# Two tiles share the weight tiles of a second layer as these are made, and a pair of tiles gets eight load buffers

## The chip, the cores and the metric

The kernel runs on one core of a Trainium2 chip. The metric is the device time of one execution in microseconds (us), smaller is better. The kernel before was timed in three runs; one further execution was recorded by the profiler, and all rows below are from it. Engines: PE is TensorE (matmuls), DVE is VectorE, ACT is ScalarE, POOL is GpSimd, and SP issues nearly all DMAs.

## The reference

Chunked attention over 8 x 8 heads of 576 positions, its 4608 tokens of 512 features, and then two dense two-layer networks, one after the other:

```python
scores = np.matmul(q_c, k_c.transpose(0, 1, 2, 4, 3)) / np.sqrt(D)     # chunks of 64
attn = np.exp(scores - np.max(scores, axis=-1, keepdims=True))
out = np.matmul(attn / (np.sum(attn, axis=-1, keepdims=True) + 1e-09), v_c)
x = out.transpose(0, 2, 1, 3).reshape(B * S, H * D)                     # 4608 x 512
h = x @ w_in                                                            # 512 -> 2048
x = (np.maximum(h, 0.0) + alpha * np.minimum(h, 0.0)) @ w_out           # 2048 -> 512
g = x @ w_gate                                                          # 512 -> 1536
y = (g * (1.0 / (1.0 + np.exp(-g))) * (x @ w_val)) @ w_out2             # 1536 -> 512
```

## The kernel before

**Tiles and products.** The 4608 tokens are nine tiles of 512. An operand in f32 is split into a high and a low part, and a product takes three matmuls of 128 x 512 (`mm3`). Weights come in a wide form; `convert` loads one block into a `raw` buffer and rebuilds it in a buffer `c` (one ACT and three DVE instructions), `whole` and `make` split it into the parts that matmuls read (buffers `w`, or `cw` for halves), and `Layer.put` stores these in DRAM (`l_in`, `l_out`, `l_b`, `l_out2`), from where `Layer.get` and `load` bring them back for later tiles. Two tiles together, a pair, are multiplied by seven products of half the size each way instead of eight (`layer1`, `layer2`); these need sums of blocks of the weights (made by `sums`, parts 5, 6, 3, 7) and sums and differences of blocks of the input (made by `operands`). A tile alone uses `plain1` and `plain2`.

**Stages**, in the order of the code and with their time in the profiled execution: attention of the first tiles (0 to 88 us); the first layer of tiles 0 and 1, `plain1` (to 181); the second layer of tile 0, `plain2`, which makes the tiles of w_out, stores them, and writes the rebuilt blocks to `cd` (to 228); the second layer of tile 1 with the stored tiles (to 276); layer 1 of pair (2,3), `mlp_a(2)` (to some 385), while `out_sums` reads `cd` back and makes the sums for w_out; layer 2 of that pair, `mlp_a2(2)` (to 495); tile 8 alone (to some 611); pair (4,5) (to 780), with `out2_quad` making the parts of w_out2; the second network for tile 0 (to 885), for the pairs (1,2) (to 1067) and (3,4) (to 1274); pair (6,7) of the first network (to 1435); the second network for (5,6) (to 1623) and (7,8). Attention of later tiles (`heads`) lies beside the matmuls of these stages.

**What sets the order.** A planner, `Program.order`, gives each instruction a place on its engine from written costs, dependencies and due times; matmuls of the products keep the order of the code ("main" items), everything else is put where a due time and free buffers allow. `after=` holds an item back until a named item has been placed. The engines then run their lists in order and wait by semaphores.

**Buffers that matter here.** `h`: 2, for activations, and for results on their way to `x2d` (`to_x2`). `t`: 5, for sums, for `t = x12 - x11` in `operands`, and for chunks of output on their way to DRAM (`e` in `to_out`). `c`: 3, for rebuilt weight blocks. `raw`: 2 double buffers, whose four halves also serve as load buffers. `xin`: 4 load buffers. `xin8` is `xin` with the halves of `raw`: 8. `w`: 7 whole weight tiles. PSUM banks: X0, X1, W0, W1, Y0, Y1, a0, a1.

**Steps that the change touches.** `operands` (L479) loads the blocks of a pair into `ring` and makes 14 operands `op` (each an ACT copy and a DVE difference). With a ring of 4 it does the whole of kt = 0 and then kt = 1; with 8 it loads the upper blocks of both first. Only the calls with `xin8` have 8: `mlp_b` and `mlp_a(6)`. `to_out` (L765) collects four blocks of a tile, transposes them on PE into banks a0 and a1 in four chunks of 128 tokens, copies each chunk to a buffer `e` and stores it. `to_x2` (L714) copies or adds a result into `h` and stores it. L229 is the copy in `copy_`, L234 the add in `add2`, L526 to L528 are the three matmuls of `mm3`: one line for many places, so the names of the tiles tell them apart.

Of the kernel before, what the change touches and what calls it, by code (L numbers as in the profile page):

```python
# [17 lines left out]
P = 128  # L18
# [123 lines left out]
def attention_moe_moe2(ctx, tc, q, k, v, w_in, w_out, alpha, w_gate, w_val, w_out2, out):  # L142
# [31 lines left out]
    NB = 512  # L174
# [44 lines left out]
    cd = dram.tile([4 * JA, P, NB], F32, name="cd")  # L219
# [78 lines left out]
    def convert(src, into=None):  # L298
# [7 lines left out]
        dma(NB * 8 * P, lambda: nsp.dma_start(out=dst, in_=src), [], rk)  # L306
# [172 lines left out]
    def operands(xd, name, i, ring):  # L479
# [169 lines left out]
    def plain2(js, col, banks, weights, natural=False):  # L649

        for m in range(2 * js):
            j, r = divmod(m, 2)
            c = 2 * r + col
            t, tk = ops.next()
            split(t[:, 0], t[:, 1], gts[j][c], NB, [("g", j, c)], tk + (0,), tk + (1,))
            w, wkeys = weights(m)

            def go(t=t, w=w, m=m):
                first, stop = m == 0, m == 2 * js - 1
                for a, b in enumerate(banks):  # L660
                    if natural:
                        acc = bank[b].rearrange("p (a f) -> p a f", a=2)
                        for i, (gp, wp) in enumerate(((0, 0), (0, 1), (1, 0))):
                            npe.matmul(out=acc, lhsT=t[:, gp, a * P:(a + 1) * P], rhs=w[:, :, wp, :],
                                       start=first and i == 0, stop=stop and i == 2, skip_group_check=True)
                    else:
                        mm3(bank[b], w[:, a // 2], t, slice((a % 2) * P, (a % 2 + 1) * P), NB, first, stop)
            item("PE", 12 * (NB + 32) / 2400, go, [*wkeys, tk + (0,), tk + (1,)], list(banks), main=True, lat=0.25)
# [340 lines left out]
```

## Time and profile before

| | us |
|---|---|
| median of 3 runs | 1816.07 |
| lowest and highest of them | 1810.56, 1817.45 |
| the profiled execution, its own time | 1815.11 |
| its span, first to last instruction | 1813.3 |
| PE busy in the span | 1689.6 |
| DVE busy | 1213.0 |
| ACT busy | 941.6 |
| mean granted clock of PE | 0.972 |

Busy time is a sum over the whole span; a stage that is bound by another engine or by a load shows only in the views by stretch. A clock of 1.00 is 2.4 GHz, 0.50 is 1.2 GHz; a value between is the mean over a stretch. In a timeline the bracket at a row's end is how long the engine had been idle before it and which instruction or transfer ended last before it started. Names such as `op<-xin` stand for a written tile and the tile that it is made from.

### The profile page before, as it was taken

The numbers are of one execution on the slowest core, as the hardware profiler recorded it, in microseconds if no ns is written. First come the engines' busy times: TensorE is split into PE (matmuls) and PEld (weight loads), VectorE is DVE, ScalarE is ACT, GpSimd is POOL, SyncE is SP. The second block draws the span as 40 slices with busy tenths as digits, with TensorE's granted clock in tenths as the row PEclk, the third lists the DMA queues.
The fourth block names the chain that finished last, engine by engine and source line by source line (L and its number), as shares of the span: only waits on it lengthen the run. The fifth ranks groups of instructions, "written<-read, shape, count | busy, mean of one in ns | idle before, by whom it ended". The sixth has DMA issues, their size and how long they took to land. (4 is left out here: it accounts for less than half of the span.)

```text
span 1813.3 us, 26654 instructions
## 1 busy us (share of the span) xinstructions
PE 1689.6 (93%) x9388; PEld 1365.9 (75%) x9388; DVE 1213.0 (67%) x2155; ACT 941.6 (52%) x1651; POOL 1.0 (0%) x8
## 2 busy tenths in 40 slices
PE   7998997879989799999899999999999799999998
PEld 6777876747767587878688778778778688778876
DVE  5787836789767688866576844587678444754473
ACT  5667525765354577544444542574675332643352
POOL 0000000000000000000000000000000000000000
PEclk8999998989989899999999999999999899999999
DMA  8879997988999995778665566896655665555553
GB/s 184 251 258 253 333 317 229 305 283 245 260 234 315 345 319 182 274 261 275 230 210 186 197 209 210 223 239 218 215 186 203 221 219 192 187 199 193 190 189 122
DMA packets 330805, 424.37 MB, mean 234 GB/s; under 512 B 176304, under 2 KB 196784, under 8 KB 330672
## 3 DMA queue, kind: packets, MB, share of 16 engines
q1 hardware_dynamic: 328608, 422.67, 73.1%
q8 instruction: 74, 1.21, 0.3%
q14 instruction: 59, 0.48, 0.1%
q10 hardware_dynamic: 2064, 0.01, 0.1%
HBM read 319.82 MB, written 102.76 MB: 233 GB/s over the span
## 5 line engine op out<-in xcount | busy, mean ns | idle before, releaser
L526 PE MATMUL X<-op,w 128*128 128x512 f32 x1056 | 422.8, 400 | 38.6 <-DVE h L234 11.1
L528 PE MATMUL X<-op,w 128*128 128x512 f32 x1056 | 415.8, 394 | 1.1 <-DVE op L234 1.1
L527 PE MATMUL X<-op,w 128*128 128x512 f32 x1056 | 415.4, 393 | 0.0
L229 ACT ACTIVATE op<-g 128x512 fp32r<-128x512 f32 x348 | 210.7, 629 | 135.6 <-PE X L527 47.3
L526 PEld LDWEIGHTS X<-op,w 128*128 128x128 f32 x1056 | 200.7, 190 | 94.5 <-ACT s L229 16.6
L234 DVE TENSOR_TENSOR op<-g,op 128x512 fp32r<-128x512 f32 x348 | 226.9, 685 | 36.6 <-ACT op L229 30.6
L526 PE MATMUL W<-op,w 128*128 128x512 f32 x544 | 216.6, 398 | 26.5 <-ACT op L229 12.0
L526 PE MATMUL Y<-op,w 128*128 128x512 f32 x560 | 226.2, 404 | 11.8 <-ACT h L698 7.7
L528 PEld LDWEIGHTS X<-op,w 128*128 128x128 f32 x1056 | 200.5, 190 | 45.1 <-DVE op L234 2.3
L527 PEld LDWEIGHTS X<-op,w 128*128 128x128 f32 x1056 | 201.1, 190 | 39.7
L528 PE MATMUL Y<-op,w 128*128 128x512 f32 x560 | 221.2, 395 | 0.0
L527 PE MATMUL Y<-op,w 128*128 128x512 f32 x560 | 221.1, 395 | 0.0
L528 PE MATMUL W<-op,w 128*128 128x512 f32 x544 | 215.7, 397 | 0.4 <-DVE op L234 0.4
L527 PE MATMUL W<-op,w 128*128 128x512 f32 x544 | 214.5, 394 | 0.0
L229 ACT ACTIVATE s<-X 128x512 f32<-128x512 f32 x172 | 102.6, 597 | 106.0 <-PE X L528 104.4
L234 DVE TENSOR_TENSOR h<-Y,s 128x512 f32<-128x512 f32 x78 | 53.7, 690 | 136.7 <-PE Y L528 136.5
L526 PEld LDWEIGHTS W<-op,w 128*128 128x128 f32 x544 | 103.6, 190 | 51.7 <-ACT op L229 14.9
L526 PEld LDWEIGHTS Y<-op,w 128*128 128x128 f32 x560 | 107.6, 192 | 36.8 <-ACT h L698 8.8
L706 DVE SCALAR_TENSOR_TENSOR g<-h,nalpha_sb,g 128x512 f32<-128x512 f32 x144 | 107.3, 747 | 33.9 <-ACT h L698 33.3
L528 PEld LDWEIGHTS Y<-op,w 128*128 128x128 f32 x560 | 106.9, 191 | 23.3
L527 PEld LDWEIGHTS Y<-op,w 128*128 128x128 f32 x560 | 107.5, 192 | 21.6
L528 PEld LDWEIGHTS W<-op,w 128*128 128x128 f32 x544 | 103.6, 190 | 25.7 <-DVE op L234 4.0
(127 smaller groups left out, 2024.0 us busy)
## 6 DMA issues: line engine op xcount, KB each, us to landing
w<-l_out SPq DMA_DIRECT2D x168, 512.0 KB, 3.6
w<-l_b SPq DMA_DIRECT2D x126, 512.0 KB, 4.3
w<-l_in SPq DMA_DIRECT2D x56, 512.0 KB, 4.3
w<-l_out SPq DMA_DIRECT2D x88, 256.0 KB, 5.3
l_b<-w SPq DMA_DIRECT2D x84, 256.0 KB, 3.4
l_out<-cw SPq DMA_DIRECT2D x80, 256.0 KB, 4.6
l_in<-w SPq DMA_DIRECT2D x64, 256.0 KB, 4.8
raw<-in_moe_w_out_dram SPq DMA_DIRECT2D x28, 512.0 KB, 5.5
```

The costliest lines, as they stand in the source:

```text
L229: pr.add([("ACT", act(n), lambda: na.activation(out=dst, in_=src, func=AF.Copy), False), ("DVE", dvep(n) if psum else dve1(n), lambda: nv. ...
L234: item("DVE", dve2(n), lambda: nv.tensor_tensor(out=dst, in0=a, in1=b, op=op), reads, writes, **kw)
L526: npe.matmul(out=acc, lhsT=w[:, 0, wk], rhs=x[:, 0, :n], start=first, stop=False, skip_group_check=True)
L527: npe.matmul(out=acc, lhsT=w[:, 1, wk], rhs=x[:, 0, :n], start=False, stop=False, skip_group_check=True)
L528: npe.matmul(out=acc, lhsT=w[:, 0, wk], rhs=x[:, 1, :n], start=False, stop=stop, skip_group_check=True)
L706: nv.scalar_tensor_tensor(out=g, in0=h, scalar=nal, in1=g, op0=ALU.mult, op1=ALU.add)
```

## The change

- `plain2` takes a list of columns. For each weight tile it issues the matmuls of tile 0 (banks X0, X1, W0, W1) and then those of tile 1 (banks Y0, Y1, a0, a1). The second pass over stored tiles for tile 1 is gone, with its 32 loads of 256 KB.
- The new `out_tile` converts two blocks of w_out, splits and stores them, and makes the sums 5, 6, 3, 7 at once from the blocks while they are in `c`. `out_sums` is gone, and so are the 16 writes to and 16 reads from `cd` for w_out (256 KB each); `cd` has half the size.
- `operands` always loads the upper blocks of both kt first, and every pair uses the ring of 8.
- A pair is a tuple of tiles. The second network now takes (1,2), (3,4), (5,8), (6,7).
- Chunks of output go through the 3 buffers `c` instead of the 5 buffers `t`.
- `out2_quad` holds its loads back until given main items are placed: four quads in the stage of tile 8, two in layer 1 of pair (4,5).

```diff
-    def operands(xd, name, i, ring):
+    def operands(xd, name, pair, ring):
...
-            dma(NB * 4 * P, lambda: nsp.dma_start(out=t, in_=xd[:, f, (i + c) * NB:(i + c + 1) * NB]),
-                [(name, i + c, f)], [key])
+            dma(NB * 4 * P, lambda: nsp.dma_start(out=t, in_=xd[:, f, pair[c] * NB:(pair[c] + 1) * NB]),
+                [(name, pair[c], f)], [key])
...
-        if ring.n == 4:
-            for kt in range(KD // 2):
-                lower(kt, *upper(kt))
-        else:
-            up = [upper(kt) for kt in range(KD // 2)]
-            for kt in range(KD // 2):
-                lower(kt, *up[kt])
+        up = [upper(kt) for kt in range(KD // 2)]
+        for kt in range(KD // 2):
+            lower(kt, *up[kt])
...
-    def plain2(js, col, banks, weights, natural=False):
+    def plain2(js, cols_, weights, natural=False):
...
             j, r = divmod(m, 2)
-            c = 2 * r + col
-            t, tk = ops.next()
-            split(t[:, 0], t[:, 1], gts[j][c], NB, [("g", j, c)], tk + (0,), tk + (1,))
             w, wkeys = weights(m)
+            for col, banks in cols_:
+                c = 2 * r + col
+                t, tk = ops.next()
+                split(t[:, 0], t[:, 1], gts[j][c], NB, [("g", j, c)], tk + (0,), tk + (1,))
...
-            e, ek = tring.next()
+            e, ek = cs.next()
             copy_(e[:w], bank[bk][:w], NB, [], [ek, bk])
...
-    def out_sums(j):
-        bl = sums(*old_tiles(2 * JA + 2 * j), False)
-        for p in (5, 6, 3, 7):
-            make(lay_out, (j, p), bl[p], chalves.next())
-
-    def out2_quad(j):
-        c = [z for m in (2 * j, 2 * j + 1) for z in convert(rows(w_out2, m))]
+    def out_tile(m, ahead={}):
+
+        j, r = divmod(m, 2)
+        if not r:
+            c = [convert(rows(w_out, 2 * j + i)) for i in range(2)]
+            for i in range(2):
+                ahead[2 * j + i] = t, keys = whole(*c[i])
+                for h, p in enumerate(OUT[i]):
+                    lay_out.put((j, p), t[:, h], keys[h])
+            bl = sums(*c[0], *c[1], False)
+            for p in (5, 6, 3, 7):
+                make(lay_out, (j, p), bl[p], chalves.next())
+        return ahead[m]
+
+    def out2_quad(j, after):
+        c = [z for m in (2 * j, 2 * j + 1) for z in convert(rows(w_out2, m), after=pr.mains[after])]
...
-        plain2(JA, 0, XW, partial(new_tile, lay_out, OUT, lambda j: j, partial(rows, w_out), base=2 * JA))
+        plain2(JA, [(0, XW), (1, YA)], out_tile)
         evict_x2(XW, 0)
-        plain2(JA, 1, YX, partial(stored, lay_out, OUT, lambda j: j))
-        evict_x2(YX, 1)
+        evict_x2(YA, 1)
...
-        mlp_a(2, second_quads(lay_in, lambda x: old_tiles(2 * x[1])))
+        mlp_a((2, 3), second_quads(lay_in, lambda x: old_tiles(2 * x[1])))
         heads(8, m0, 14)
-        for j in range(JA):
-            out_sums(j)
-        mlp_a2(2)
+        mlp_a2((2, 3))
...
-        for j in range(JB):
-            out2_quad(j)
-        mlp_a(4, got_in)
-        mlp_a2(4)
+        for j in range(4):
+            out2_quad(j, m0 + 6 * j)
+        m0 = len(pr.mains)
+        mlp_a((4, 5), got_in)
+        for j in range(4, JB):
+            out2_quad(j, m0 + 20 * (j - 4))
+        mlp_a2((4, 5))
...
-        mlp_b(5, got_b)
-        mlp_b(7, got_b)
+        mlp_b((5, 8), got_b)
+        mlp_b((6, 7), got_b)
```

**The order on ACT, at the start of pair (2,3).** In a row the number at the end of a name is the buffer. Before, results `h` of tile 1 are copied between operands `op` that are made from loads `xin`:

```order
L229 ACTIVATE w_5_135<-t_2_127 128x256
L229 ACTIVATE op_5_72<-xin_3_116 128x512
L229 ACTIVATE s_0_117<-W0_159 128x512
L229 ACTIVATE w_6_136<-t_3_128 128x256
L229 ACTIVATE h_0_123<-X0_157 128x512
L229 ACTIVATE op_7_74<-xin_2_115 128x512
L229 ACTIVATE op_9_76<-xin_1_114 128x512
L229 ACTIVATE h_1_124<-X1_158 128x512
L229 ACTIVATE op_3_70<-xin_0_113 128x512
L229 ACTIVATE s_1_118<-X0_157 128x512
```

After, the place where the results of tile 0 are copied out of X0 to W1:

```order
L229 ACTIVATE op_8_75<-xin_1_114 128x512
L229 ACTIVATE op_9_76<-xin_3_116 128x512
L229 ACTIVATE h_0_123<-X0_157 128x512
L229 ACTIVATE h_1_124<-X1_158 128x512
L229 ACTIVATE w_0_130<-t_2_127 128x256
L229 ACTIVATE op_10_77<-raw_0_139 128x512
L229 ACTIVATE w_1_131<-t_2_127 128x256
L229 ACTIVATE op_11_78<-raw_1_140 128x512
L229 ACTIVATE w_2_132<-t_3_128 128x256
L229 ACTIVATE h_0_123<-W0_159 128x512
L229 ACTIVATE h_1_124<-W1_160 128x512
L229 ACTIVATE w_3_133<-t_3_128 128x256
```

The operands that stood between the copies of X0 and the first `s` have moved ahead of these copies, and they are made from `raw` as well as `xin`.

**The order on ACT, at the end of pair (3,4) or (5,6) of the second network and the start of the next.** Before, at the end of (5,6):

```order
L229 ACTIVATE t_1_126<-a1_164 128x512
L229 ACTIVATE t_2_127<-a0_163 128x512
L229 ACTIVATE g6_3_108<-X1_158 128x512
L229 ACTIVATE t_3_128<-a1_164 128x512
L229 ACTIVATE t_4_129<-a0_163 128x512
L229 ACTIVATE t_0_125<-a1_164 128x512
L229 ACTIVATE t_1_126<-a0_163 128x512
L229 ACTIVATE t_2_127<-a1_164 128x512
L229 ACTIVATE op_6_73<-t_3_128 128x512
L229 ACTIVATE op_7_74<-t_4_129 128x512
L229 ACTIVATE op_2_69<-xin_1_114 128x512
L229 ACTIVATE op_3_70<-xin_3_116 128x512
```

After, at the end of (5,8):

```order
L229 ACTIVATE op_4_71<-raw_0_139 128x512
L229 ACTIVATE g6_2_107<-X0_157 128x512
L229 ACTIVATE g6_3_108<-X1_158 128x512
L229 ACTIVATE op_5_72<-raw_1_140 128x512
L229 ACTIVATE s_0_117<-W0_159 128x512
L229 ACTIVATE s_1_118<-X0_157 128x512
L229 ACTIVATE c_2_143<-a0_163 128x512
L229 ACTIVATE c_0_141<-a1_164 128x512
L229 ACTIVATE s_2_119<-X0_157 128x512
L732 ACTIVATE g0_0_81<-h_0_123 128x512
L732 ACTIVATE g0_1_82<-h_1_124 128x512
```

The operands `op` stand ahead of the copies out of a0 and a1; the copies write `c`, and there are two in place of eight before the next layer's `g`.

**The order on ACT, at the end of the kernel.** Before:

```order
L229 ACTIVATE g6_2_107<-X0_157 128x512
L229 ACTIVATE t_1_126<-a0_163 128x512
L229 ACTIVATE t_2_127<-a1_164 128x512
L229 ACTIVATE t_3_128<-a0_163 128x512
L229 ACTIVATE t_4_129<-a1_164 128x512
L229 ACTIVATE t_0_125<-a0_163 128x512
L229 ACTIVATE t_1_126<-a1_164 128x512
L229 ACTIVATE t_2_127<-a0_163 128x512
L229 ACTIVATE t_3_128<-a1_164 128x512
```

After:

```order
L229 ACTIVATE c_2_143<-a0_163 128x512
L229 ACTIVATE c_0_141<-a1_164 128x512
L229 ACTIVATE c_1_142<-a0_163 128x512
L229 ACTIVATE g6_2_107<-X0_157 128x512
L229 ACTIVATE g6_3_108<-X1_158 128x512
L229 ACTIVATE c_2_143<-a1_164 128x512
L229 ACTIVATE c_0_141<-a0_163 128x512
L229 ACTIVATE c_1_142<-a1_164 128x512
L229 ACTIVATE c_2_143<-a0_163 128x512
L229 ACTIVATE c_0_141<-a1_164 128x512
L229 ACTIVATE c_1_142<-a0_163 128x512
L229 ACTIVATE c_2_143<-a1_164 128x512
```

Ten copies through three buffers stand where eight went through five.

## Rows read from the trace of the kernel before

**Rows 1.** The page, part 1: busy time, share of the span, instructions.

```profile
PE 1689.6 (93%) x9388; PEld 1365.9 (75%) x9388; DVE 1213.0 (67%) x2155; ACT 941.6 (52%) x1651; POOL 1.0 (0%) x8
```

**Rows 2.** Stretches: from:to, length, busy by engine (x), PE clock, DMA share, GB/s.

```profile
181.00:228.00 47.00, 45.24 (x240) 37.26 (x234) 37.90 (x68) 25.35 (x45) 0.00 (x0) 1.00 0.98 336
228.00:276.00 48.00, 46.93 (x234) 38.16 (x234) 16.98 (x34) 11.53 (x23) 0.00 (x0) 1.00 0.93 312
276.00:310.00 34.00, 25.60 (x92) 19.48 (x91) 22.02 (x43) 20.64 (x41) 0.00 (x0) 0.80 0.76 233
310.00:380.00 70.00, 57.11 (x266) 45.16 (x266) 56.24 (x126) 51.07 (x108) 0.00 (x0) 0.96 0.93 303
380.00:410.00 30.00, 24.63 (x155) 16.71 (x157) 26.01 (x52) 17.28 (x34) 0.00 (x0) 0.86 0.83 250
400.00:450.00 50.00, 47.84 (x357) 36.89 (x348) 47.26 (x86) 28.87 (x49) 0.00 (x0) 1.00 0.75 221
495.00:535.00 40.00, 34.07 (x224) 26.90 (x224) 28.63 (x56) 22.91 (x46) 0.00 (x0) 0.91 0.92 224
535.00:600.00 65.00, 59.10 (x446) 46.72 (x446) 46.39 (x100) 28.27 (x59) 0.00 (x0) 0.97 1.00 313
600.00:622.00 22.00, 13.33 (x42) 9.86 (x42) 18.37 (x33) 12.64 (x24) 0.00 (x0) 0.77 0.97 349
```

**Rows 3.** Timeline of PE: start, us, instruction, [idle before <- ended by].

```profile
283.69 0.80 PE L526 MATMUL X<-op,w 128*128 128x512 f32 x1 [7.19 <-ACT h L229]
...
600.14 0.80 PE L526 MATMUL W<-op,w 128*128 128x512 f32 x1 [2.35 <-DMA w<-l_out]
...
617.45 0.80 PE L526 MATMUL W<-op,w 128*128 128x512 f32 x1 [6.84 <-ACT h L229]
...
885.28 0.80 PE L526 MATMUL W<-op,w 128*128 128x512 f32 x1 [5.35 <-ACT w L229]
...
1445.68 0.79 PE L526 MATMUL X<-op,w 128*128 128x512 f32 x1 [10.00 <-ACT op L229]
...
1625.75 0.50 PE L526 MATMUL W<-op,w 128*128 128x512 f32 x1 [2.60 <-ACT op L229]
...
1631.05 0.50 PE L526 MATMUL X<-op,w 128*128 128x512 f32 x1 [0.69 <-ACT s L229]
```

**Rows 4.** Timeline of ACT, 276 to 287 us.

```profile
279.71 0.63 ACT L229 ACTIVATE op<-xin 128x512 fp32r<-128x512 f32 x1 [1.90 <-DMA xin<-x1d]
...
283.04 0.60 ACT L229 ACTIVATE h<-X 128x512 f32<-128x512 f32 x1 [1.91 <-DMA x2d<-h]
```

**Rows 5.** Busy time by stretch, at three joints between pairs.

```profile
878.00:892.00 14.00, 7.95 (x24) 5.41 (x23) 6.74 (x14) 6.63 (x13) 0.00 (x0) 0.76 0.56 189
1066.00:1076.00 10.00, 6.59 (x22) 4.31 (x22) 7.93 (x13) 6.17 (x11) 0.00 (x0) 0.83 0.66 200
1434.00:1450.00 16.00, 6.00 (x18) 4.34 (x17) 7.27 (x12) 5.55 (x10) 0.00 (x0) 0.68 0.53 168
```

**Rows 6.** Chain of waits, 1430:1452 and 1616:1634: start, us, what.

```profile
1433.40 5.73 DMA x2d<-h
...
1439.15 3.56 DMA raw<-x2d
...
1619.60 3.40 DMA out_dram<-t
```

**Rows 7.** Chain of waits, the end.

```profile
1801.24 0.23 PE X L528
...
1805.73 2.40 DMA out_dram<-t
...
1808.23 0.60 ACT t L229
```

**Rows 8.** Groups of DVE instructions, 181 to 276 us: busy us, mean ns.

```profile
L234 DVE TENSOR_TENSOR op<-g,op 128x512 fp32r<-128x512 f32 x24 | 15.7, 684 | 2.2 <-ACT op L229 2.2
...
L234 DVE TENSOR_TENSOR t<-c,c 128x256 f32<-128x256 f32 x3 | 1.3, 419 | 0.0
```

More of the change, by code (lines that the diff above doesn't have):

```diff
@@ L296, in rows, with convert @@
         return w[m * P:(m + 1) * P, :]
-    def convert(src, into=None):
+    def convert(src, into=None, after=None):
         raw, rk = raws.next()
@@ L647, in plain1, with go @@
                 outs(qs[m // 2], 2 * (m % 2) + col, acc, b, None)
-    def plain2(js, col, banks, weights, natural=False):
+    def plain2(js, cols_, weights, natural=False):
         for m in range(2 * js):
             j, r = divmod(m, 2)
-            c = 2 * r + col
-            t, tk = ops.next()
-            split(t[:, 0], t[:, 1], gts[j][c], NB, [("g", j, c)], tk + (0,), tk + (1,))
             w, wkeys = weights(m)
[L658 to L668, printed above, removed]
+            for col, banks in cols_:
+                c = 2 * r + col
+                t, tk = ops.next()
+                split(t[:, 0], t[:, 1], gts[j][c], NB, [("g", j, c)], tk + (0,), tk + (1,))
+                def go(t=t, w=w, m=m, banks=banks):
+                    first, stop = m == 0, m == 2 * js - 1
+                    for a, b in enumerate(banks):
+                        if natural:
+                            acc = bank[b].rearrange("p (a f) -> p a f", a=2)
+                            for i, (gp, wp) in enumerate(((0, 0), (0, 1), (1, 0))):
+                                npe.matmul(out=acc, lhsT=t[:, gp, a * P:(a + 1) * P], rhs=w[:, :, wp, :],
+                                           start=first and i == 0, stop=stop and i == 2, skip_group_check=True)
+                        else:
+                            mm3(bank[b], w[:, a // 2], t, slice((a % 2) * P, (a % 2 + 1) * P), NB, first, stop)
+                item("PE", 12 * (NB + 32) / 2400, go, [*wkeys, tk + (0,), tk + (1,)], list(banks), main=True, lat=0.25)
     def stored(layer, parts, name, m):
@@ L712, in leaky, with to_x2 @@
         item("DVE", dve2(n), join, rd, [gk, tk, *wr], port=not psum)
-    def to_x2(m, c, acc, b, s, n, i0):
+    def to_x2(m, c, acc, b, s, n, pair):
         t, tk = hring.next()
@@ L763, in store_rows, with to_out @@
         dma(w * NB * 4, store, [ek], [])
-    def to_out(m, c, acc, b, s, n, n0, got):
+    def to_out(m, c, acc, b, s, n, pair, got):
         t, tk = spare[(2 * (c >= 2) + m) + 4 * (c % 2)]
@@ L810, in second_quads, with new_tile @@
         return get
-    def new_tile(layer, parts, name, src, m, keep=None, base=0):
+    def new_tile(layer, parts, name, src, m, keep=None):
         j, r = divmod(m, 2)
@@ L880, in attention_moe_moe2, with mlp_a, mlp_a2, mlp_b @@
                                               for h in range(2))])
-        def mlp_a(i, weights, ring=xin):
-            o = operands(x1d, "x1", i, ring)
+        def mlp_a(pair, weights):
+            o = operands(x1d, "x1", pair, xin8)
             layer1(qa, NB, o, weights, leak)
-        def mlp_a2(i):
-            layer2(JA, NB, lay_out, partial(to_x2, n=NB, i0=i))
-        def mlp_b(i, weights, between=lambda: None):
-            o = operands(x2d, "x2", i, xin8)
+        def mlp_a2(pair):
+            layer2(JA, NB, lay_out, partial(to_x2, n=NB, pair=pair))
+        def mlp_b(pair, weights, between=lambda: None):
+            o = operands(x2d, "x2", pair, xin8)
             layer1(qb, NB, o, weights, act_b)
             between()
-            layer2(JB, NB, lay_out2, partial(to_out, n=NB, n0=i * NB, got={}))
+            layer2(JB, NB, lay_out2, partial(to_out, n=NB, pair=pair, got={}))
         def got_in(x, p):
@@ L950, in attention_moe_moe2 @@
                                       keep=lambda m: keep[qb[m // 2]][m % 2]), act_b)
-        plain2(JB, 0, XW, partial(stored, lay_out2, OUT, lambda j: j), natural=True)
+        plain2(JB, [(0, XW)], partial(stored, lay_out2, OUT, lambda j: j), natural=True)
         for a, b in enumerate(XW):
-            e, ek = tring.next()
+            e, ek = cs.next()
             copy_(e, bank[b], NB, [], [ek, b])
```

24 lines of the change are left out of this document (12 added, 12 removed).

## The prediction

> **What bounds the kernel now.** I read the page's first part first: TensorE is busy for 1689.6 of 1813.3 us [rows 1], so the most that any reordering can give is the other 124 us and what matmuls lose at the lower of the two clocks (1.2 instead of 2.4 GHz). The order of instructions shows the same 7354 instructions on PE before and after, so the change adds and removes no matmul: everything is in PE's waits and clock. I then read busy time and clock by stage. The reader should see where PE is full (181 to 276 us, 45.24 of 47 and 46.93 of 48, clock 1.00) and where it isn't: 276 to 410 us and 495 to 622 us [rows 2]. A timeline of PE then shows what ended each long wait, and that the rest sits at the joints between pairs of tiles: 885, 1069, 1275, 1445, 1626 us [rows 3, 5]. Last, the chain of waits at two joints and at the end [rows 6, 7].
>
> **The profiled run.** It took 1815.11 us for a span of 1813.3; the median is 1816.07. I sum against 1815.11; the 1 us to the median is less than the runs differ among themselves.
>
> **Part 1: layer 1 of pair (2,3), 276 to 410 us.** PE idles there 34 - 25.60, 70 - 57.11 and 30 - 24.63 us, 26.7 in all [rows 2]. The clocks 0.80, 0.96 and 0.86 stand for 6.8 + 2.8 + 4.2 = 13.8 us; a part of the slow time is idle and counted already, so I take 10. The longest wait, 7.19 us at 283.69, ends on ACT's `h<-X` [rows 3], and ACT's timeline shows why: that copy stands behind `op<-xin`, which waited for a load, and then waited itself for its `h` buffer's store [rows 4]. The change gives the pair 8 load buffers instead of 4 and orders the operands by use, so all of them are made while the shared stage still runs. The later waits stand where out_sums and its reads of cd share DVE, ACT and DMA with this layer (DVE 56.24 and ACT 51.07 of 70, DMA 0.93 of 310 to 380 [rows 2]); all of that moves ahead. What remains: eight evictions through two `h` buffers instead of four behind four banks. W0, which the first product of the pair needs, is the third to be copied and so waits for the store of X0. That store took 5.73 us at another place [rows 6]; with a copy of 0.60 before and after [rows 4], less the 2.7 us (12 matmuls of 0.23 [rows 7]) by which X0 is ready before the stage ends, PE waits about 4 us, and the clock drops for about 1.7. With 4 us for small waits some 10 us stay. Gain 36.7 - 10 = 26; between 18 (a second such wait at Y0, and the small waits twice over) and 33 (W0's store as quick as an output store, 3.40 [rows 6], and no other wait).
>
> **Part 2: tile 8 and the start of pair (4,5), 495 to 622 us.** Idle 5.9 + 5.9 + 8.7 = 20.5 us, and about 7 of clock (0.91, 0.97, 0.77) [rows 2]. The wait of 6.84 us at 617.45 is the same pattern as at 283.69 and goes with the 8 buffers and the order of use. The wait at 600.14 (2.35 us), and a shorter one at 607.60, end on loads of weights [rows 3], with the DMA engines at 1.00 and 0.97 [rows 2]. The order shows that the loads and stores placed between main matmuls 1440 and 2160 (tile 8 and layer 1 of pair (4,5)) are 63.7 MB before and 63.2 after: the traffic of this stretch isn't relieved. The same two `h` buffers also keep an eviction wait of 4 to 6 us. So I take only 8 of 27; bounds 0 and 15. The two quads of w_out2 that are put off into layer 1 of pair (4,5) add DVE and ACT work there; I price it at 2 us, 0 to 8.
>
> **Part 3: the joints.** At 1434 to 1450, after mlp_a2 of (6,7), PE waits 10.00 us [rows 3]: the chain goes from `x2d<-h` (5.73) to `raw<-x2d` (3.56) to the operands [rows 6], since pair (5,6) needs tile 6 that was stored just then. The next pair is now (5,8), both stored long before, so its operands can be ready. The clock of 0.68 over 16 us is 5.1 us, some 3 of it in the idle time [rows 5]; gain 10 + 2.1, less 0.69 for the wait that every pair has at its start [rows 3]: 11.5. At 1069, 1275 and 1626 PE waits 2.52, 2.45 and 2.60 us ([rows 3] has the last of the three): eight output copies take all five `t` buffers, `t` is also what `op<-t` is made from, and a buffer comes free when its store lands, 3.40 us on [rows 6]. Each costs 2.5 and 10 x (1 - 0.83) = 1.7 us of clock [rows 5]. Copies now use the three `c` buffers, so the operands no longer wait for them; two chunks go at the joint, the rest beside the next pair's matmuls. That is -4 each at 1069 and 1626. At 1275 the order puts all eight chunks ahead of the copies that the first products of layer 1 need; the waits for three buffers there may be as long as the one that goes: -1 (-4 to +3). At 885 the wait of 5.35 and some 2.4 of clock [rows 3, 5] shrink to 1.7: -6. Sum -26.5, bounds -32 and -17.
>
> **Part 4: the end.** Before, the last matmul of a product ends at 1801.5, and the last copy at 1808.8, 7.4 us later [rows 7]: eight chunks and five buffers. In the new order ten chunks stand behind the last product, and three buffers turn over once in copy + store + handover, 0.6 + 3.40 + 0.1 = 4.1 us by row 1619.60, or 3.1 us by the 2.40 of the end itself [rows 6, 7]. The tenth copy is three turns behind the first, which starts 0.5 us after the last product: it ends at 0.5 + 3 x 4.1 + 0.6 = 13.4, or at 10.4. Cost +6 or +3. I take +5: the chunks in the middle of the end run like the longer row.
>
> **Part 5: the shared stage, 181 to 276 us.** It drops tile 1's 32 loads of half tiles and the 4 MB each way of cd, but PE was full while these ran (46.93 of 48, DMA 0.93), so they were hidden, and taking them away gives nothing there. What it adds is DVE work: 37.90 + 16.98 = 54.9 us before [rows 2]; the new order has between main matmuls 384 and 768 88 DVE instructions of 512 columns and 69 of 256, at 0.684 and 0.419 at most 60 + 29 = 89 us [rows 8], against PE's 92. Cover for this is thin. One stretch shows both engines so full (DVE 47.26 and PE 47.84 of 50, 400 to 450 us [rows 2]). I take +4; bounds 0 and +13 (DVE at 0.85 of the time: 89 / 0.85 = 105 us, less the 95 it has, and some clock).
>
> **Sum.** -26 - 8 + 2 - 26.5 + 5 + 4 = -49.5: 1815.1 - 49.5 = 1765.6, **1766 us**.
>
> **Rivals.** (a) *The early gains don't come*, since DMA or DVE sets the time up to 700 us. For it: DMA 0.92 to 1.00 from 495 to 622 with the same bytes, DVE nearly full in the shared stage; against it: the two longest waits there end on copies queued behind loads, not on weights. Then part 1 gives 8, part 2 nothing, part 5 costs 8, and the joints and the end stay: -8 + 2 - 26.5 + 5 + 8 = -19.5, 1796. The Trainium skill ("Perfetto Trace Analysis", What "DMA-bound" means) counts full DMA engines as a bound of their own; by that the stretch at DMA 1.00 keeps its time whatever order the engines have. The trace agrees only for the two waits that end on weights. (b) *Three output buffers hold PE at each joint*: six of the eight chunks wait two turns of 4.1 us, and the two banks they sit in stop the next product, 8 us at each of the four joints, -49.5 + 33: 1815.1 - 16.5 = 1799. For it: the new order at 1275; against it: elsewhere the chunks lie between the next pair's matmuls. The Trainium skill ("Perfetto Trace Analysis", Optimization Strategy) reads a gap that repeats as a sign of too few buffers; the three repeated waits at 1069, 1275 and 1626 agree, and five buffers becoming three speaks against this change. (c) *Slower*: DVE can't keep up in the shared stage and PE waits at each weight tile often enough that its clock stays at 1.2 GHz through these 384 matmuls. These take 384 x 0.23 = 88 us at the full clock and as much again at half: -49.5 + 88, about 1854. It decides from the point where waits as long as those after which the clock fell (2.35 to 2.6 us) recur at every pair of weight tiles [rows 3].
>
> **How the numbers follow.** Forecast 0.62, (a) 0.2, (b) 0.11, (c) 0.04; 0.03 is left for a time below. The forecast's own bounds are 1815.1 - 33 - 15 - 32 + 3 = 1738 and 1815.1 - 18 + 8 - 17 + 6 + 13 = 1807, not all at once: 1744 to 1790. The range has to take in (a) and (b): 1742 to 1800. A measurement of this kernel can tell some 0.5%, 9 us, from no change. Faster by more than that: the forecast, and nearly all of (a) and (b), 0.9; same 0.05, what (a) and (b) leave when they come together; slower 0.05, (c) and a little beside.
>
> **What would show it.** Part 1: no wait over 5 us on PE within the 134 us after the shared stage, a clock above 0.95. Part 2: the wait on `h<-W` halved, waits on `w<-l_out` kept. Part 3: no wait of 10 us before pair (5,8); at the other joints no wait on `op`, and small ones on `c`. Part 4: ten copies after the last product, 10 to 13.5 us. Part 5: DVE at 0.85 to 0.95 of the shared stage with PE's clock 1.00. The forecast is wrong if PE shows waits at each weight tile of the shared stage, if the DMA engines stay full into pair (4,5) and PE waits for weights there, or if the operands of a pair still start late.

## The result, and the profile after

The changed kernel takes 1745.71 us (median of 4 runs, 1741.51 to 1748.46), the kernel before 1813.32 us (median of 4, 1810.46 to 1817.45). The ratio is 0.9623, with a 95% interval of 0.9589 to 0.9658: 67.6 us faster. The forecast was 1766 us with a range of 1742 to 1800: right in direction, inside the range, but 18 us short of the gain, and the sum came out near for partly wrong reasons.

The page's first line for the kernel after, as [rows 1]; the span is 1741.2 us, so PE idles 80 us instead of 124. Its busy time fell too, by 28.5 us for the same 9388 matmuls: its mean granted clock is 0.989 where it was 0.972.

```profile
PE 1661.1 (95%) x9388; PEld 1352.7 (78%) x9388; DVE 1215.6 (70%) x2156; ACT 935.7 (54%) x1649; POOL 1.0 (0%) x8
```

Stretches of the kernel after (from:to, length, busy by engine (x), PE clock, DMA share, GB/s). The first two are the shared stage, the next two are layer 1 of pair (2,3), the last is the start of pair (4,5):

```profile
180.70:228.00 47.30, 47.30 (x238) 39.02 (x237) 41.49 (x84) 28.54 (x58) 0.00 (x0) 1.00 0.81 287
228.00:270.60 42.60, 41.36 (x183) 33.93 (x181) 35.54 (x75) 20.80 (x44) 0.00 (x0) 1.00 0.78 269
270.60:310.00 39.40, 34.45 (x137) 27.28 (x138) 24.51 (x50) 24.55 (x48) 0.00 (x0) 0.91 0.87 267
310.00:380.00 70.00, 67.20 (x407) 54.21 (x406) 60.93 (x111) 51.33 (x99) 0.00 (x0) 1.00 0.72 213
572.00:590.00 18.00, 8.72 (x27) 6.71 (x28) 10.10 (x20) 7.70 (x16) 0.00 (x0) 0.72 0.82 305
```

In the shared stage PE is as full as in [rows 2], with its clock at 1.00, and DVE is busy 41.49 + 35.54 = 77.0 of 89.9 us, 0.86. From 310 to 380 us PE now has 67.20 of 70 us where it had 57.11. The last row is the worst place that stayed.

Timeline of PE in the kernel after (start, us, instruction, what ended the idle time before it), as [rows 3]:

```profile
270.64 0.50 PE L522 MATMUL W<-op,w 128*128 128x512 f32 x1 [1.28 <-ACT h L229]
...
286.37 0.80 PE L522 MATMUL X<-op,w 128*128 128x512 f32 x1 [3.56 <-DVE h L234]
...
580.60 0.79 PE L522 MATMUL W<-op,w 128*128 128x512 f32 x1 [9.28 <-ACT h L229]
...
850.18 0.50 PE L522 MATMUL X<-op,w 128*128 128x512 f32 x1 [0.69 <-ACT s L229]
...
1293.75 0.50 PE L522 MATMUL X<-op,w 128*128 128x512 f32 x1 [1.69 <-DVE h L234]
...
1383.90 0.50 PE L522 MATMUL X<-op,w 128*128 128x512 f32 x1 [0.69 <-ACT s L229]
```

The wait of 7.19 us, ten us into pair (2,3), is gone; PE waits 1.28 us at the pair's first matmul now, and a new wait of 3.56 us stands 16 us into the pair. The one of 6.84 us at the start of pair (4,5) has grown to 9.28. The joints at 850 and 1384 us show only the 0.69 us that every pair has; the 10.00 us before pair (5,6) and the 5.35 us at 885 are gone.

PE's matmuls stand in the same number in the same stages in both kernels (pair (5,8) in the place of (5,6), pair (6,7) in that of (7,8)), so the start of the same matmul can be compared in the two traces. The profiled runs, in us, times between such points:

| stretch | before | after | change | forecast |
|---|---|---|---|---|
| start to the end of the second layer of tiles 0 and 1 | 273.7 | 270.6 | -3.1 | +4 |
| pair (2,3), both layers | 212.7 | 183.9 | -28.8 | -26 |
| tile 8, to some us into pair (4,5) | 139.0 | 134.8 | -4.2 | -8 |
| rest of pair (4,5) | 149.8 | 152.1 | +2.3 | +2 |
| tile 0 of the second network, with the joint at 885 | 127.7 | 120.2 | -7.5 | -6 |
| pair (1,2) and the joint at 1069 | 184.2 | 174.8 | -9.4 | -4 |
| pair (3,4) and the joint at 1275 | 206.1 | 198.8 | -7.3 | -1 |
| pair (6,7) and the joint at 1445 | 169.6 | 163.8 | -5.8 | -11.5 |
| next pair of the second network and the joint at 1626 | 179.7 | 170.2 | -9.5 | -4 |
| last pair, to its last matmul | 158.6 | 159.1 | +0.5 | 0 |
| from there to the end of the span | 12.2 | 12.9 | +0.7 | +5 |
| sum | 1813.3 | 1741.2 | -72.1 | -49.5 |

One profiled run is not the same as the next where attention and its loads lie beside the matmuls. Runs of kernels that have the same code there differ by up to 7 us in the first stretch (269.0 to 275.9), from 180.1 to 185.7 in pair (2,3), and from 132.9 to 137.3 in that of tile 8. So -28.8 is clear, -4.2 is not far outside, and -3.1 says little. The second layer of tiles 0 and 1 by itself, from its first matmul to the first of pair (2,3), repeats: 89.9 us in each of these runs, against 92.4 us before.

### The profile page after: what moved, and what is told of

Its sections match the earlier page's. It is cut to its first block, busy times and chain, and to the rows that moved or that the text cites. A ratio compares the mean times of both kernels' runs of the same rounds, so it can differ in the third digit from the quotient of the medians.

```text
span 1741.2 us, 26558 instructions
## 1 busy us (share of the span) xinstructions
PE 1661.1 (95%) x9388; PEld 1352.7 (78%) x9388; DVE 1215.6 (70%) x2156; ACT 935.7 (54%) x1649; POOL 1.0 (0%) x8
## 4 chain that ended last, share of the span: by engine, by line
PE 52%; DMA 2%; DVE 2%; ACT 1%; issue 0%; ACTq 0%; SPq 0%; DVEq 0%
PE X L522 9%; PE X L523 9%; PE X L524 9%; PE W L522 5%; PE W L524 5%; PE W L523 5%; PE Y L523 2%; PE Y L522 2%; PE Y L524 2%; DMA raw<-in_moe_w_gate_dram 1%; PE X L661 1%; PE W L661 1%; DMA raw<-in_moe_w_val_dram 1%; PE a L781 1%; PE a L465 0%
## 5 line engine op out<-in xcount | busy, mean ns | idle before, releaser
L522 PE MATMUL X<-op,w 128*128 128x512 f32 x1024 | 407.8, 398 | 19.1 <-DVE h L234 12.7
L523 PE MATMUL X<-op,w 128*128 128x512 f32 x1024 | 400.8, 391 | 0.0
L524 PE MATMUL X<-op,w 128*128 128x512 f32 x1024 | 400.6, 391 | 0.0
L522 PEld LDWEIGHTS X<-op,w 128*128 128x128 f32 x1024 | 193.2, 189 | 70.6 <-DVE h L234 17.3
L524 PEld LDWEIGHTS X<-op,w 128*128 128x128 f32 x1024 | 193.4, 189 | 41.1
L522 PE MATMUL W<-op,w 128*128 128x512 f32 x544 | 214.0, 393 | 10.6 <-ACT h L229 10.6
L523 PEld LDWEIGHTS X<-op,w 128*128 128x128 f32 x1024 | 193.5, 189 | 37.8
L524 PE MATMUL W<-op,w 128*128 128x512 f32 x544 | 212.4, 390 | 0.0
L523 PE MATMUL W<-op,w 128*128 128x512 f32 x544 | 212.2, 390 | 0.0
L522 PEld LDWEIGHTS W<-op,w 128*128 128x128 f32 x544 | 102.4, 188 | 33.2 <-ACT h L229 11.4
```

The lines of the kernel that those rows point to most:

```text
L522: npe.matmul(out=acc, lhsT=w[:, 0, wk], rhs=x[:, 0, :n], start=first, stop=False, skip_group_check=True)
L523: npe.matmul(out=acc, lhsT=w[:, 1, wk], rhs=x[:, 0, :n], start=False, stop=False, skip_group_check=True)
L524: npe.matmul(out=acc, lhsT=w[:, 0, wk], rhs=x[:, 1, :n], start=False, stop=stop, skip_group_check=True)
```

## The experiments

All runs below are edits of the changed kernel; a time is the median of 4 to 6 runs. The theory was the forecast's own list of causes; each of the first five takes one part of the change back.

**The pair order.** Only the tuples of the last two pairs are changed back.

```diff
-        mlp_b((5, 8), got_b)
-        mlp_b((6, 7), got_b)
+        mlp_b((5, 6), got_b)
+        mlp_b((7, 8), got_b)
```

> The changed kernel (1745.7 us) with the second network's last pairs as (5,6), (7,8) again. Theory: the pair order alone removed the joint after mlp_a2 of (6,7); PE waits some 10 us there again, behind the store and the load of tile 6's blocks, and the clock drops once: +11 us, about 1757. Rival: the operands' order of use and the free buffers removed it, and the pair order does nothing: 1746, no wait over 3 us there.

Measured: 1756.9 us (1755.6 to 1760.7), +11.2. The wait on PE and the chain of waits in this kernel:

```profile
1393.61 0.79 PE L522 MATMUL X<-op,w 128*128 128x512 f32 x1 [9.86 <-ACT op L229]
```

```profile
1381.47 5.70 DMA x2d<-h
...
1387.19 3.46 DMA raw<-x2d
```

The store of 5.70 us, the load of 3.46 us and the operands stand before PE as in [rows 6]. The theory holds and the rival falls: with 8 buffers and everything else in place the whole wait is back, so the pair order removes it. The end of this kernel is longer as well, 14.3 us from the last product's last matmul instead of 12.9; part 4 below comes back to it.

**The buffers of the output chunks.** Chunks go through the five `t` again, in `to_out` and for tile 0.

```diff
-            e, ek = cs.next()
+            e, ek = tring.next()
```

> The changed kernel with the output chunks in the five buffers t again. Theory: the chunks in t held the operands; the joints after (1,2), (3,4) and (5,8) cost 8 to 10 us each again (eight transposes paced by copies, a wait of 2.5 us on op, the clock at 0.83), and the end gets 1 to 2 us shorter: +20 to +27, about 1768. Rival: the joints went because the planner had other room (pairs, operands), and the buffer of the copy does not matter: within 5 us of 1746.

Measured: 1775.9 us (1773.1 to 1780.0), +30.2. The first matmuls after the joints at 1069, 1275 and 1626 in this kernel's timeline of PE:

```profile
1039.15 0.79 PE L522 MATMUL W<-op,w 128*128 128x512 f32 x1 [2.96 <-ACT op L229]
...
1245.93 0.60 PE L522 MATMUL W<-op,w 128*128 128x512 f32 x1 [2.39 <-ACT op L229]
...
1585.94 0.80 PE L522 MATMUL W<-op,w 128*128 128x512 f32 x1 [3.63 <-ACT op L229]
```

The waits on `op` are back at all three joints, and at the joint of tile 0 the wait on `w` too (5.78 us at 854.11). The stretches of the table lose 7.1, 10.7, 7.1 and 11.3 us at the four joints, pair (6,7) gains 5.5 and the end 3.5. The theory holds, with more than it gave: this small part of the change is its largest single gain. Three buffers, which rival (b) of the forecast held to be too few, cost at most the two amounts that come back; these also hold what the transposes take at their new place, and no run parts the two.

**The eight load buffers.** Pairs (2,3) and (4,5) use the four `xin` and the old order of operands.

```diff
-        up = [upper(kt) for kt in range(KD // 2)]
-        for kt in range(KD // 2):
-            lower(kt, *up[kt])
+        if ring.n == 4:
+            for kt in range(KD // 2):
+                lower(kt, *upper(kt))
+        else:
+            up = [upper(kt) for kt in range(KD // 2)]
+            for kt in range(KD // 2):
+                lower(kt, *up[kt])
...
-            o = operands(x1d, "x1", pair, xin8)
+            o = operands(x1d, "x1", pair, ring)
```

> The changed kernel with four load buffers and the old order of operands for pairs (2,3) and (4,5). Theory: the wait of 7 us on the copy of h at the start of pair (2,3) comes back with its clock, +9 to +12 us there; at the start of (4,5) the wait of 9.3 us stays as it is, since the raw halves were not free there: about 1756. Rival a: the shared stage alone removed the wait at (2,3), within 3 us of 1746. Rival b: with four buffers of xin alone the start of (4,5) gets faster, since it no longer stands behind the conversions that hold raw: -5 there.

Measured: 1747.4 us (1742.4 to 1749.6), +1.7, inside the spread of the runs. PE at the starts of (2,3) and (4,5):

```profile
274.07 0.50 PE L526 MATMUL W<-op,w 128*128 128x512 f32 x1 [1.81 <-ACT h L229]
...
579.45 0.79 PE L526 MATMUL W<-op,w 128*128 128x512 f32 x1 [9.10 <-ACT h L229]
```

1.81 us instead of 1.28, and 9.10 instead of 9.28. The theory falls, rival a holds: where the second layer is shared, four load buffers would have done, and at (4,5) eight or four make no difference. Rival b falls too.

**The shared stage.** Two passes again, with `cd`, `out_sums` and the stored tiles; the 8 buffers and all else stay.

```diff
-        plain2(JA, [(0, XW), (1, YA)], out_tile)
+        plain2(JA, [(0, XW)], partial(new_tile, lay_out, OUT, lambda j: j, partial(rows, w_out), base=2 * JA))
         evict_x2(XW, 0)
-        evict_x2(YA, 1)
+        YX = ("Y0", "Y1", "X0", "X1")
+        plain2(JA, [(1, YX)], partial(stored, lay_out, OUT, lambda j: j))
+        evict_x2(YX, 1)
...
+        for j in range(JA):
+            out_sums(j)
         mlp_a2((2, 3))
```

> The changed kernel with the second layer of tiles 0 and 1 in two passes again: stored weight tiles for tile 1, blocks of w_out written to cd and read back, sums made beside the pair (2,3). Theory: the 8 buffers keep the start of (2,3) free, but the later waits between 300 and 410 us come back (some 18 us idle and 6 of clock before), and the two-pass stage is 3 us longer: +20 to +27, about 1768. Rival: the 8 buffers and the order of operands made most of the gain there: +3 to +8, about 1751.

Measured: 1771.4 us (1770.3 to 1775.1), +25.6. PE's longest waits from 277 to 380 us, and the two stretches:

```profile
281.99 0.80 PE L522 MATMUL X<-op,w 128*128 128x512 f32 x1 [3.54 <-ACT h L229]
...
361.87 0.50 PE L522 MATMUL X<-op,w 128*128 128x512 f32 x1 [3.68 <-DVE h L234]
...
378.36 0.87 PE L457 MATMUL a<-ident,pp 128*128 128x128 f32 x3 [7.75 <-DVE pp L234]
```

```profile
277.00:310.00 33.00, 28.44 (x107) 22.36 (x106) 21.72 (x43) 20.83 (x41) 0.00 (x0) 0.84 0.80 237
310.00:380.00 70.00, 56.29 (x263) 44.74 (x262) 54.68 (x121) 49.21 (x105) 0.00 (x0) 0.93 0.90 296
```

The theory holds, the rival falls. Pair (2,3) takes 206.0 us here, 183.9 with the shared stage and 212.7 in the kernel before. The first wait is 3.54 us instead of 7.19, but the stage ahead is longer here, 96.5 us against 92.4 before. From the first matmul of that stage to the end of pair (2,3) it is 305.1 us before, 302.4 here and 273.8 with the shared stage: in a two-pass kernel the 8 buffers are worth some 3 us, less than runs of one kernel differ, and the shared stage some 29. With it `out_sums`, its reads and its `cw` are out of a layer in which PE waits for DVE (PE is busy for 56.29 of 70 us here, as 57.11 in [rows 2]).

**The hold on the loads of w_out2.** All six quads stand in the stage of tile 8, without `after`.

```diff
-        for j in range(4):
-            out2_quad(j, m0 + 6 * j)
-        m0 = len(pr.mains)
+        for j in range(JB):
+            out2_quad(j)
...
-        for j in range(4, JB):
-            out2_quad(j, m0 + 20 * (j - 4))
```

> The changed kernel with all six quads of w_out2 in the stage of tile 8 and without the hold on their loads, as before. Theory: the hold costs nothing and wins little, since the wait at the start of pair (4,5) is set by the copies of h that stand behind operands: the two quads come out of layer 1 of (4,5), -1 to -3 us there, and the stage of tile 8 gets +2 to +5: 1745 to 1750. Rival: the hold is what kept the loads of tile 8's weights in time; without it the waits on loads of weights come back at the end of tile 8 with their clock, +6 to +10: about 1754.

Measured: 1746.0 us (1740.1 to 1753.9), no change that can be told. The wait at the start of (4,5) is 11.23 us, and pair (4,5) isn't shorter. PE waits for no load of weights in the stage of tile 8, so the hold isn't what removed those of [rows 3], and what did stays open; the rival falls, and with it the 2 us of the forecast for the two quads that were moved, as far as this can be told.

The five parts add up: 11.2 + 30.2 + 1.7 + 25.6 + 0.2 = 68.9 us, against 67.6 us for the whole change; three of them make it, the pair order, the buffers of the chunks and the shared stage.

**The wait that stayed: the start of pair (4,5).** ACT's timeline in the kernel after, 562 to 582 us:

```profile
574.01 0.63 ACT L229 ACTIVATE op<-raw 128x512 fp32r<-128x512 f32 x1 [0.97 <-DMA raw<-x1d]
574.55 1.06 ACT L229 ACTIVATE h<-X 128x512 f32<-128x512 f32 x2
577.81 0.63 ACT L229 ACTIVATE op<-raw 128x512 fp32r<-128x512 f32 x1 [2.19 <-DVE raw L234]
579.95 1.23 ACT L229 ACTIVATE h<-W 128x512 f32<-128x512 f32 x2 [1.51 <-DMA x2d<-h]
```

The last matmul of tile 8 starts at 570.9. Its first result is copied out of X at 574.55, behind an operand that waits for its load, and the copy out of W, which the next product needs, waits until 579.95 for the store of an `h` buffer: two causes, 3.7 and 5.4 us. The loads are late although there are 8 buffers: four of these are the halves of `raw`, in which the quads of w_out2 are rebuilt until 563 us, so the loads into them are issued from 563.5 to 568.3 us only. Three runs try the two causes. The first changes one number of the planner, the time that it counts from an operand's load to its landing:

```diff
-                [(name, pair[c], f)], [key])
+                [(name, pair[c], f)], [key], lat=5.0)
```

> The changed kernel with one number of the planner changed: it now plans 5.0 us instead of 2.2 us from the issue of an operand's load to its landing. Theory: the 9.3 us wait at the start of (4,5) has two parts, some 3.5 us in which the copy of X0 to h stands behind operands whose loads are late, and some 5 us for the turn of the two h buffers; the planner can only move the first, so the wait falls to 6 to 9 us: 1742 to 1746. Rival: the late loads are the whole of it, and the wait falls under 3 us: about 1737.

Measured: 1741.5 us (1739.1 to 1747.3). PE's wait, and ACT at the same place:

```profile
578.74 0.79 PE L522 MATMUL W<-op,w 128*128 128x512 f32 x1 [5.69 <-ACT h L229]
```

```profile
572.19 1.07 ACT L229 ACTIVATE h<-X 128x512 f32<-128x512 f32 x2
...
578.09 1.21 ACT L229 ACTIVATE h<-W 128x512 f32<-128x512 f32 x2 [4.32 <-DMA x2d<-h]
```

The copy out of X is no longer late (the last matmul of tile 8 starts at 572.66), and the turn of the two `h`, 5.9 us from one copy to the other, makes the wait that is left. As the theory has it, the planner's number moves only the smaller part. That this gains time is not shown: 1741.5 us is as much as the fastest of the changed kernel's eight runs (1741.5 to 1750.8), and the changed kernel's own wait at this place is anything from 6.12 to 9.60 us in the five profiled runs whose code is the same up to there. In the one with 6.12, that of the pair order, the copy out of X isn't late either; the turn of `h` is 5.3 to 6.2 us in all five. The second run takes W0 and W1 of tile 8 out through two buffers `t`, so that they need not wait for `h`:

```diff
-                to_x2(f % 2, 2 * (f // 2), bank[b], b, None, NB, (i,))
+                to_x2(f % 2, 2 * (f // 2), bank[b], b, None, NB, (i,), late if f > 1 else hring)
...
-        evict_x2(XW, 8)
+        evict_x2(XW, 8, tring)
```

> The changed kernel with W0 and W1 of tile 8 copied out to two buffers t instead of waiting for the two h. Theory: the turn of the two h buffers is the larger part of the 9.3 us wait; without it PE waits 1 to 4 us at the start of (4,5), and the clock drops for less: -6 to -10, about 1738. Rival: the loads of the operands set the start, the copies only come last: the wait ends on op instead of on h and stays at 7 us or more, 1744 to 1747.

Measured: 1764.8 us (1759.4 to 1766.7), 19 us worse; neither side expected that. PE and ACT at the start of (4,5):

```profile
600.85 0.80 PE L522 MATMUL W<-op,w 128*128 128x512 f32 x1 [25.50 <-ACT op L229]
```

```profile
570.70 1.16 ACT L229 ACTIVATE t<-W 128x512 f32<-128x512 f32 x2
...
600.17 1.23 ACT L229 ACTIVATE op<-t 128x512 fp32r<-128x512 f32 x2 [1.09 <-DVE t L234]
```

W is copied at 570.70, as early as could be, but now `op<-t` is made at 600.17 only: buffers are given out in the order of the code, the results of tile 8 stand ahead of the next pair's operands in the ring `t`, and all that takes a `t` behind them can't start until tile 8 has ended. Between them and the operands stand the sums of w_out2: DVE rebuilds six of the eight blocks of its first four quads from 579 to 599 us, where in the changed kernel all eight are done at 563. It is the fault of the kernel before at its joints, made anew at another place. The third run takes buffers that nobody wants: of `g`, tile 8 alone leaves half unused, and the last ones are written late in the next layer.

```diff
-        t, tk = hring.next()
+        t, tk = into or hring.next()
...
-        evict_x2(XW, 8)
+        evict_x2(XW, 8, [(gts[j][c], ("g", j, c)) for j in (6, 7) for c in (1, 3)])
```

> The changed kernel with the four results of tile 8 copied to four buffers g that layer 1 of (4,5) writes last, instead of the two h, so that no copy waits for a store and no operand waits for a copy. Theory: with the turn of the h buffers gone the wait of 9.3 us at the start of (4,5) falls to 3 to 5 us, what the operands' late loads leave, and the clock drops for less: -5 to -8, about 1739. Rival: the late loads set the start alone, the wait then ends on op and stays above 7 us: 1743 to 1746.

Measured: 1734.4 us (1733.8 to 1742.4), ratio to the kernel before 0.9576 (0.9544 to 0.9608). PE and ACT at the same place:

```profile
570.43 0.56 PE L522 MATMUL W<-op,w 128*128 128x512 f32 x1 [1.81 <-ACT g L229]
```

```profile
568.76 1.14 ACT L229 ACTIVATE op<-raw 128x512 fp32r<-128x512 f32 x2
569.80 0.58 ACT L229 ACTIVATE g<-W 128x512 f32<-128x512 f32 x1
570.28 0.59 ACT L229 ACTIVATE g<-X 128x512 f32<-128x512 f32 x1
```

All four results leave within 2.1 us, and the wait is 1.81 us, well under the 6.12 to 9.60 of the changed kernel's code: the theory holds, with a larger gain than it gave. The turn of the two `h` buffers, the larger part of the wait, is gone. The loads aren't late here either: the planner put the rest in another order, and the last load into `raw` is issued at 561.4 us, 6.8 us before the last matmul of tile 8, instead of 3.1. So this run doesn't show what late loads would cost without the turn of `h`.

**The end.** The last pair's chunks go through the five `t`, all others through `c`.

```diff
-        mlp_b((6, 7), got_b)
+        mlp_b((6, 7), got_b, ring=tring)
```

> The changed kernel with the last pair's output chunks in the five buffers t instead of the three c. Theory: in the changed kernel the three buffers cost a turn at the end; five give what the kernel with t for all chunks showed, 9.4 us from the start of the last product's last matmul to the end of the span instead of 12.9: -3 to -4, about 1742. Rival: the end is paced by the transposes and copies, ten chunks of 1.3 us either way: no change within 1 us at the end.

Measured: 1742.7 us (1741.0 to 1749.9), which the spread of the runs hides; in the trace the end after the last matmul is 11.4 us instead of 12.9. Both sides are half right: 1.5 us of the end are the three buffers; 2 more are the two chunks that lie over from the pair before, which the kernel with `t` for all chunks hasn't (9.4 us).

**Together.** With buffers `g`, the five `t` at the end and the planner's 5.0 us:

> The changed kernel with the buffers g for tile 8's results, the five buffers t for the last pair's output, and 5.0 us planned for operands' loads. Theory: the three add up: start of (4,5) -6 to -9, start region of loads -1 to -2, end -1.5: 1734 to 1738. Rival: moving operands for the later loads only shifts waits into the stage of tile 8, as the run with 5.0 alone showed (+5.1 there, -3.6 at the start): 1739 to 1742.

Measured: 1738.4 us (1732.8 to 1743.9). Without the planner's 5.0 us:

> The changed kernel with tile 8's results in four buffers g and the last pair's output in the five buffers t, the planner's numbers as they were. Theory: the two gains lie at different places and add: -8 at the start of (4,5) and its clock, -1.5 at the end against the changed kernel: 1732 to 1736. Rival: the gain of the buffers g alone was partly the spread of runs: 1737 to 1741.

Measured: 1736.9 us (1728.7 to 1744.2), ratio 0.9589 (0.9554 to 0.9623). The changed kernel itself, run again beside the first of these and the buffers `g`:

> The changed kernel itself once more, to compare the two above on the same chip: 1742 to 1748.

Measured: 1746.3 us (1744.9 to 1750.8). The three versions with buffers `g` (1734.4, 1738.4, 1736.9) can't be told apart; their medians are 8 to 12 us under those of the changed kernel, though single runs overlap (up to 1744.2 against 1741.5 and more). The traces say where: the stretch of tile 8 with the start of (4,5) takes 124.1 to 126.4 us in them, against 132.9 to 137.3, and the end is 1.5 us shorter in the last two.

## Why the prediction was right or wrong

**Part 1, pair (2,3): the size right (28.8 against 26), half of the reason wrong, so the near size is partly luck.** The forecast gave the start to the 8 load buffers. The run with four shows that they bring nothing there once the stage is shared, and the run with two passes that they bring little without it. What the stage before does to the loads and to ACT decided whether the operands came in time; that it is its lighter traffic (DMA 0.81 and 0.78 busy, where [rows 2] have 0.98 and 0.93) is argued and not shown. The remaining wait at the start was put at 4 us and is 1.28: 21 matmuls, 4.8 us, stand behind X0's last one in the stage, and not the 12 of the forecast (ACT copies X at 264.63 us, the stage's last matmul starts at 268.97). The eight evictions through two `h` cost PE at a later place, the "second such wait" of the lower bound. PE's 3.56 us at 286.37 end on an `h` of layer 1. On DVE it stands behind two others, which had to wait for the stores of tile 1's results:

```profile
282.42 0.69 DVE L234 TENSOR_TENSOR h<-Y,s 128x512 f32<-128x512 f32 x1 [0.81 <-DMA x2d<-h]
283.57 0.69 DVE L234 TENSOR_TENSOR h<-W,s 128x512 f32<-128x512 f32 x1 [0.46 <-DMA x2d<-h]
```

The clock is 0.91 up to 310 us, less than the 0.95 that was expected, and 1.00 behind. The part on `out_sums` was right, as the run with two passes shows.

**Part 2, tile 8 and the start of (4,5): the failed step.** The forecast let the 6.84 us go with "the 8 buffers and the order of use" and added that an eviction wait of 4 to 6 us stays. The eviction wait was sized rightly, 5.4 us of the 9.28; what did not go is the rest, since half of the 8 buffers are still in use for w_out2 when the pair's loads are due. So of the -8 + 2 = -6 us only -1.9 came. [rows 4] had both causes, a load and a store of `h`; the store was the larger here, and the change left it. The loads of weights did stop ending waits, which may be the small gain; why they did is open. (The clocks of these three stretches stand for 10.6 us, of which the forecast counted 7 without a reason; its 8 us don't hang on it.)

**Part 3, the joints: the mechanism right, the term mis-sized.** Price by row was 2.5 us of waiting and 1.7 of clock, 4.2 us; each of three joints gave 9.6. What was left out is in the kernel before, between the last matmul of one pair and the first of the next:

```profile
1618.35 1.04 PE L784 MATMUL a<-ident,g 128*128 128x128 f32 x8
1619.63 1.30 PE L784 MATMUL a<-ident,g 128*128 128x128 f32 x8 [0.25 <-ACT t L229]
1621.10 1.18 PE L784 MATMUL a<-ident,g 128*128 128x128 f32 x8 [0.16 <-ACT t L229]
1622.49 0.66 PE L784 MATMUL a<-ident,g 128*128 128x128 f32 x4 [0.21 <-ACT t L229]
```

PE is "busy" here with 28 transposes at the pace of ACT's copies, 4.8 us that stand in no gap but hold the next matmul. After, at the joint of the last two pairs, that of before at 1626 us, the first product of the next pair follows without a break:

```profile
1553.91 0.39 PE L524 MATMUL X<-op,w 128*128 128x512 f32 x1
1554.14 0.39 PE L522 MATMUL W<-op,w 128*128 128x512 f32 x1
```

The transposes go between later matmuls. They come back in part: 2.3 us in pair (3,4), and 5.5 us in pair (6,7), where the eight chunks go from 1277 to 1297 us, ahead of copies for which products wait (1.69 us at 1293.75). So the joint at 1275 came to -9.6 + 5.5 against -1, that at 1069 to -7.3 against -4. The joint at 1445 was right to the quarter of a microsecond: 11.3 against 11.5.

**Part 4, the end: +0.7 against +5.** Ten chunks and three buffers were right; the price of a turn was not. ACT's copies in the kernel after, and the last steps of its chain:

```profile
1729.19 1.09 ACT L229 ACTIVATE c<-a 128x512 f32<-128x512 f32 x2 [19.03 <-PE a L781]
...
1731.97 2.01 ACT L229 ACTIVATE c<-a 128x512 f32<-128x512 f32 x3
1734.78 1.99 ACT L229 ACTIVATE c<-a 128x512 f32<-128x512 f32 x3 [0.79 <-PE a L781]
1737.53 0.60 ACT L229 ACTIVATE c<-a 128x512 f32<-128x512 f32 x1 [0.76 <-DMA out_dram<-c]
```

```profile
1728.47 0.24 PE X L524
...
1735.40 2.02 DMA out_dram<-c
```

The store takes 2.02 us here, less than both rows [rows 6, 7], and the chain waits for a store once. Ten copies take 9.4 us from the last matmul, under the lower bound of 10.4 and 2.0 us more than the eight before; from the last copy to the end of the span it is 3.1 us instead of 4.5. The row from the end itself was the nearest and should have been taken. What the forecast missed besides is that the new pair order takes tile 8 out of the last pair. Tile 8 holds the last 64 positions of eight sequences, so each of its chunks goes out in two stores of 64 rows. The stores of the end, before (1800 to 1812 us), after (1729 to 1741 us), and in the run with the old pair order (1738 to 1756 us):

```profile
out_dram<-t SPq DMA_DIRECT2D x8, 128.0 KB, 2.3
out_dram<-t SPq DMA_DIRECT2D x4, 256.0 KB, 2.7
...
out_dram<-c SPq DMA_DIRECT2D x10, 256.0 KB, 2.0
...
out_dram<-c SPq DMA_DIRECT2D x6, 256.0 KB, 2.1
out_dram<-c SPq DMA_DIRECT2D x8, 128.0 KB, 2.4
```

With tile 8 at the end and three buffers (the run with the old pair order), copies wait for a store four times, the tenth ends 10.8 us after the last matmul, inside the forecast's 10.4 to 13.4, and the end is 14.3 us. So the lower price of a turn was right for the pair order of before; under the new one the three buffers cost 1.5 us, as the run with five shows.

**Part 5, the shared stage: nothing lost, against +4.** The stage itself takes 89.9 us where it took 92.4. DVE needed 77.0 us and not 89: the count was right (157, and 158 in the trace), but 11 of the 88 with 512 columns take 0.42 us, and those that follow each other without a wait overlap. Two with 512 columns in the kernel after:

```profile
577.09 1.29 DVE L234 TENSOR_TENSOR raw<-raw,xin 128x512 f32<-128x512 f32 x2
```

That is 1.29 us, not 2 x 0.69. The removed loads of tile 1 were hidden but for those 2.4 us at most: the gain of the shared stage lies in pair (2,3).

**The rivals.** (a) had the size of the stretch up to (4,5) right and the cause wrong: what held the start of (4,5) was the turn of `h` and not full DMA engines, for with buffers `g` the stretch is 8 us or more shorter with the same bytes to move. On part 1 it was wrong. (b) named a cost of which at most 7.8 us came, in two places, a quarter of its price. (c) didn't come: the clock stayed at 1.00 in the shared stage.

The terms' errors, in the order of the parts, are -2.8, +4.1, -12.5 (with the last pair's +0.5), -4.3 and -7.1 us; the joints are more than half of the -22.6 us by which the trace passes the sum.

## What to carry to other kernels

A pool that gives buffers out in the order of the code ties what comes next to the last user's store: results on their way out belong in buffers that the next stage's inputs don't need, and two uses of one small pool are worth more attention than its size. When pricing a joint, take the time from the last matmul of one part to the first of the next, not the gap that the profile marks; an engine that does small work at another's pace counts as busy. When a wait has two causes on one queue, price both before saying that one edit removes it. And when the order of tiles changes, look at what the tile that comes last does differently.

## What the runs showed of the hardware that was not expected

- An output store of 256 KB lands in 2.02 us at the end of the kernel, where nothing but such stores moves, and in 3.40 us at a joint; a store of the same size to `x2d` took 5.70 and 5.73 us when loads were in flight. Two stores of 128 KB in the place of one of 256 KB land no sooner: 2.3 and 2.4 us each (medians), against 2.0 to 2.7.
- DVE instructions on 512 columns that follow each other without a wait take 1.28 to 1.29 us for two, though one alone shows 0.68 to 0.69.
- Between runs of one kernel the time differs by up to 0.9% (1728.7 to 1744.2 us for the version with buffers `g` and five `t`); in the traces the differences lie in attention and in the stages up to tile 0 of the second network, while the stretches from pair (1,2) on repeat within 0.1 us in kernels that have the same code there, but for that of pair (6,7), which differs by up to 0.6 us.
